# Asking earlier for the keys of step 17, and own buffers with early loads for both halves of the output weights

## The chip, the cores and the metric

The kernel runs on one core of one Trainium2 chip. The metric is the device time of one execution in microseconds, as the median of several runs. A core has five engines that work side by side, each through its own queue in order: TensorE (PE, matrix products), VectorE (DVE), ScalarE (ACT), GpSimd (POOL) and SyncE (SP, which here only asks for transfers). All loads and stores are made by 16 DMA engines; SyncE, ScalarE and GpSimd ask for them.

## The reference, cut to what matters

Attention over a window of neighbours and over block summaries, and behind it a gated layer with two further products. Shapes: 4 batches, 8 heads, 768 rows of 64; 3072 tokens of 512; inner width 1024.

```python
k_sum = k.reshape(B, H, nb, 32, D).max(axis=3)
v_sum = v.reshape(B, H, nb, 32, D).mean(axis=3)
scores_l = where(|i - j| < 16, scale * q @ k.T, -1e9)
scores_s = scale * q @ k_sum.T + log(32)
a = softmax(concatenate([scores_l, scores_s]))
x = a @ concatenate([v, v_sum])          # as (3072, 512)
out = ((x @ w1) * (x @ w2) @ w3) @ w_out
```

## The kernel before, in words

All work is in 32-bit floats; a product is made of three passes over high and low halves of its operands (`products`, L123). The tokens are cut into 6 units of 512 and the heads into 4 pairs, which makes 24 attention steps, numbered 0 to 23. A step loads queries and keys (`load_scores`, L336) and values (`load_values`, L319), adds block summaries to the keys (`gather`, L361, on GpSimd, called through `fill`), makes scores (L376), a softmax over them (`reduce`, `expose`, `invert`, `normalize`, L385 to L414), transposes (L434) and outputs (`outputs`, L449). Queries and keys have two buffers each, so the loads of step p + 2 take the buffers of step p once its scores are done.

The weights w3 and w_out are multiplied with each other at the start (`fold_weights`, L226), into eight tiles `wp`, so that the network is two gate products, their product, and one output product. The first two units go through it in a plain form (`gate`, `project`; the results are copied into tiles `o` and stored, L553 to L556). The other four go in two rounds through a form with seven products of half the size in place of eight (`gates`, `project_fast`, `lanes`, L721 to L753). For that form sums of blocks of the weights are needed. `sums_of_gates` makes them for the gate weights and `sums_of_output` (L948) for the output weights, in two halves c = 0 and 1: `stationary` (L666) loads four blocks `wr` of a half from DRAM (`pR`, written earlier by `spill_high` and `join_wp`, L928 and L931), adds them on VectorE (L690, L692, L696, L701), splits each sum into two parts `sp` (L680 on ScalarE, L121 on VectorE) and stores them (L686). The products in `lanes` go to four accumulators that L759 (ScalarE) and L761 (VectorE) empty into `tmp` and `hr`.

The order of TensorE's and GpSimd's work is written out by hand. Steps 8 to 15 are handled by `lump` (L1288), one at a time, and steps 16 to 23 by `two_steps` (L1325), two at a time. Between the parts of a step, `run` (L997) lets the network go on up to a given number of columns. While it does, `tend` (L982) advances small pieces of side work, one at a time: first the list `tasks`, then the list `background`, whose first entry has to end before the next begins. What SyncE asks for, and what VectorE and ScalarE do outside of the parts with a fixed order, is put into the queues by a scheduler before the run: it takes what it thinks ready, by order in the program, and can take an instruction well ahead of its place.

Names and lines that the change touches:

- `keep_raw` (L466) copies the outputs of steps 8 to 23 into tiles `xraw`. Those of steps 16 to 19 are two tiles with the tag `raw` (two buffers, otherwise used by `load_keys` and `load_blocks`); those of steps 8 to 11 are two with the tag `wf` (six buffers, shared with the softmax tiles `sm`).
- `stationary` has for the output weights four small tiles with the tag `pt` (four buffers). The same tag holds the tiles `o` and `g` of the plain form. Both halves c use it, one after the other.
- `sums_of_output` is put into `background` at the first and the second pair of `two_steps` (`LATER`, L1269). Its loads (L954) are asked for when the background work comes to it.
- `lump(15)` asks for queries and keys of step 17 at its end (L1321), and lets GpSimd add the summaries (L1322).

Of the kernel before, what the change touches and what calls it, by code (L numbers as in the profile page):

```python
# [11 lines left out]
F32 = mybir.dt.float32  # L12
# [8 lines left out]
P = 128  # L21
# [52 lines left out]
def attention_moe(ctx, tc, qG, kW, kT, vP, vW, vB, mask, w1, w2, w3T, wo, out, outT):  # L74
    nc = tc.nc
    B, NPAIR, _, S = kT.shape
    S -= PAD
    NB = S // BLOCK
    U = TOKENS
# [8 lines left out]
    NC = DM // P  # L88
    FQ = w1.shape[2] // 2 // NC
    NF = w1.shape[0] * FQ // P  # L90
# [4 lines left out]
    DH = DO // 2  # L95
# [4 lines left out]
    sb = ctx.enter_context(tc.tile_pool(name="sb", bufs=2))  # L100
# [11 lines left out]
    wp = [sb.tile([P, 2, DO], F32R, name=f"wp{i}", tag="wp", bufs=NF) for i in range(NF)]  # L112

    wS = [[tc.dram_tile([P, 2, KH * FQ], F32, name=f"wS{k}_{q}") for q in range(NQ)] for k in range(NK)]
    pS = {k: [tc.dram_tile([P, 2, 2 * DH], F32, name=f"pS{k}_{c}") for c in range(NF // 4)] for k in range(2, NK - 1)}
    pR = [tc.dram_tile([P, 2, 2, DO], F32, name=f"pR{c}") for c in range(NF // 4)]
# [3 lines left out]
    def low(eng, dst, src, hi):  # L120
        eng.tensor_tensor(dst, src, hi.bitcast(F32), ALU.subtract)  # L121
# [214 lines left out]
    def load_scores(u, p):  # L336

        q = sb.tile([P, U], F32, name="q")
        k = sb.tile([P, NBLK, COLS], F32, name="k")
        eng = nc.gpsimd if u > LAST_UNITS or u == LAST_UNITS and p > 1 else nc.sync  # L340
        eng.dma_start(q, qG[p, :, u * U : (u + 1) * U])
        if u:
            eng.dma_start(k, kW[p, :, u * NBLK : (u + 1) * NBLK])
        return q, k
# [40 lines left out]
    def reduce(u, h, sc, sm, mx):  # L385

        for i in ORDER:
            blk = (u * NBLK + i) % BLOCKS
            j = h * NBLK + i
            nc.vector.tensor_tensor_reduce(  # L390
                out=sm[:, j],
                in0=sc[h][:, i * KR : (i + 1) * KR],
                in1=mask_sb[:, 0 if blk == 0 else 2 if blk == BLOCKS - 1 else 1],
                op0=ALU.add,
                op1=ALU.min,
                scale=-SCALE,
                scalar=3.0e38,
                accum_out=mx[:, 0, j : j + 1],
            )
# [66 lines left out]
    def keep_raw(po, u, c):  # L466

        n, half = divmod(u, 2)
        if (n, half) not in raws:
            if half:  # L470
                home = {"tag": "w12", "bufs": 8} if n == 1 else {"tag": "ring", "bufs": RING}
                t = sb.tile([P, NC, U], F32, name="xraw", **home)
                raws[n, half] = [t[:, i] for i in range(NC)]
            else:
                home = {"tag": "wf", "bufs": 6} if n == 1 else {"tag": "raw", "bufs": 2}
                two = [sb.tile([P, 2, U], F32, name="xraw", **home) for _ in range(NC // 2)]
                raws[n, half] = [two[i // 2][:, i % 2] for i in range(NC)]
        nc.scalar.copy(raws[n, half][c], po[:, :U])
        kept[n, half] = kept.get((n, half), 0) + 1
# [175 lines left out]
    def staggered(works):  # L655

        active = []
        while works or active:
            if works:
                active.append(works.pop(0))  # L660
            active = [work for work in active if next(work, 0)]
            yield 1

    stored = set()

    def stationary(name, load, to_dram, home, apart=False):  # L666


        if apart:
            t = [[sb.tile([P, 512], F32, name="wr", tag="pt", bufs=4) for _ in range(2)] for _ in range(2)]  # L670
        else:
            whole = sb.tile([P, 2, 2, 512], F32, name="wr", tag="ring", bufs=RING)
            t = [[whole[:, i, j] for j in range(2)] for i in range(2)]
        yield from load(t)
        (a11, a12), (a21, a22) = t
        yield 1

        def finished(k, raw):
            to = sb.tile([P, 2, 512], F32R, name="sp", **home)
            nc.scalar.copy(to[:, 0], raw)  # L680
            yield 1
            low(nc.vector, to[:, 1], raw, to[:, 0])
            yield 1
            yield 1
            yield 1
            nc.sync.dma_start(to_dram(k), to.bitcast(F32))  # L686
            stored.add((name, k))

        works = []
        nc.vector.tensor_tensor(a22, a21, a22, ALU.add)  # L690
        yield 1
        nc.vector.tensor_tensor(a21, a11, a21, ALU.subtract)  # L692
        works.append(finished(2, a22))
        next(works[0])
        yield 1
        nc.vector.tensor_tensor(a11, a22, a11, ALU.subtract)  # L696
        works.append(finished(5, a21))
        next(works[0])
        next(works[1])
        yield 1  # L700
        nc.vector.tensor_tensor(a12, a12, a11, ALU.subtract)  # L701
        if apart:
            yield from staggered([*works, finished(4, a11), finished(3, a12)])
            return

        yield from staggered(works)
        for _ in range(3):
            yield 1
        yield from staggered([finished(4, a11), finished(3, a12)])
# [53 lines left out]
    xT, raws, kept, hT, tasks, background = {}, {}, {}, {}, [], []  # L763
# [183 lines left out]

    def sums_of_output(c):  # L948

        def load(t):  # L950
            for h in range(2):
                for i in range(2):
                    to = t[i][h].rearrange("p (j d) -> p j d", d=DH)
                    nc.sync.dma_start(to, pR[c][:, h, :, i * DH : (i + 1) * DH])  # L954
            yield from range(1, 5)

        return stationary("p%d" % c, load, lambda k: pS[k][c], {"tag": "wp", "bufs": NF}, True)

    def network():
        for u in range(2):  # L960
# [21 lines left out]
    def tend():  # L982


        some = False
        for works in (tasks, background):
            while works:
                n = next(works[0], 0)
                if n > 0:
                    return True  # L990
                if n < 0:
                    break
                works.pop(0)
                some = True
        return some

    def run(columns):  # L997

        while given[0] < columns:
            n = next(stream, 0)  # L1000
            if n <= 0:
                if n == 0 or not tend():
                    return
                continue
            given[0] += n
            if given[0] >= tended[0]:
                tended[0] = max(tended[0] + 4.5 * U, given[0])
                tend()

    def place(s):  # L1010
        return divmod(s, NPAIR)
# [3 lines left out]
    def fetch(s):  # L1015
        if s < NS:
            inputs[s] = load_scores(*place(s))

    def fetch_values(s):
        if s < NS:  # L1020
            values[s] = load_values(*place(s))
# [5 lines left out]
    def fill(s):  # L1027
        if s < NS:
            gather(*place(s), inputs[s][1])
# [159 lines left out]
    with tc.manual_schedule(engines={engines.SP}):  # L1189
        start_loads(0)  # L1190
        active, pairs, t = [], [], [-1]
        while units or active or pairs or delayed or WORK or t[0] <= FIRST[-1]:
# [20 lines left out]
            if t[0] in FIRST[: NPAIR + 1]:  # L1213
                n = FIRST.index(t[0])
# [37 lines left out]
    SINGLE = LAST_UNITS * NPAIR  # L1252
# [3 lines left out]
    PAIRS = range(SINGLE // 2, NS // 2)  # L1256
# [3 lines left out]
    def begins(m):  # L1260
# [6 lines left out]
        15: [lambda: flow_in(4), lambda: moving_x(1, 2)],  # L1267
    }
    LATER = {  # L1269
        (PAIRS[0], 0): [lambda: background.append(sums_of_output(0))],  # L1270
        (PAIRS[0], 1): [lambda k=k: moving_x(1, k) for k in range(3, NK)],
        (PAIRS[0] + 1, 0): [lambda: background.append(sums_of_output(1))],
    }

    for i in range(NF):
# [12 lines left out]
    def lump(p):  # L1288

        if p == NFIRST:  # L1290
            load_batch()
            fill(p)
        else:
            fetch_means(*place(p - 1), values[p - 1])
            fetch(p + 1)
        with tc.manual_schedule(engines=VECTOR):
            t, home = sms.pop(p - 2)
            pt = evacuate(transposes(t), "V" if p in (12, 13) else "A", home)
            u, sm, mx, sc = begin(p)
            reduce(u, 0, sc, sm, mx)  # L1300
            if p > NFIRST + 1:
                expose(0, sm, mx)
                reduce(u, 1, sc, sm, mx)
        run(given[0] + (24 if p == NFIRST + 1 else 18) * U)
        with tc.manual_schedule(engines=VECTOR):
            finish_step(p - 2, pt, **SPARE)
            if p <= NFIRST + 1:
                expose(0, sm, mx)
                reduce(u, 1, sc, sm, mx)
            expose(1, sm, mx)  # L1310
            invert(mx)
            normalize(sm, mx)
            fill(p + 1)
            reduce_batch()
        fetch_values(p)
        for work in EXTRA.get(p, ()):
            work()
        run((given[0] + UP_TO[p]) / 2)
        load_batch()
        if p == SINGLE - 1:  # L1320
            fetch(p + 2)  # L1321
            fill(p + 2)  # L1322
        run(UP_TO[p])

    def two_steps(m):  # L1325
# [133 lines left out]
```

## Time and profile before

| | us |
|---|---|
| median of 3 runs | 514.2 |
| lowest and highest run | 513.1, 516.83 |
| the profiled execution | 517.44 |
| its span, first to last instruction | 515.7 |
| TensorE busy in the span | 486.8 |
| VectorE, ScalarE, GpSimd busy | 357.2, 317.3, 62.5 |

The rows further below come from the profiled execution. Times in them are microseconds from the start of the span. A row of a timeline has its start, its length, the engine, the line of the kernel, the operation, what it writes and reads, and how many instructions are merged in it; in square brackets stands how long the engine had been idle before it and what ended that. SPq is the queue of SyncE; its length is that of the asking, not of the transfer. A row of the waits has the total in us, how often, and the longest. Shares and clocks are in tenths or as fractions; a granted clock of 1.00 is 2.4 GHz, and the lower level is 1.2 GHz.

### The profile page before, as it was taken

What the parts mean: (1) busy time and instruction counts of PE and PEld (TensorE: products, weight loads), DVE (VectorE), ACT (ScalarE), POOL (GpSimd) and SP (SyncE); (2) the same over time, 40 slices, a digit from 0 to 9 for tenths busy, and PEclk for the clock granted to TensorE, in tenths of its full rate; (3) what the DMA queues carried; (4) which work ended last, traced back from release to release, by engine and by line L of the source; (5) the groups of instructions that cost most, each with busy time, mean ns of one, the idle gap of its engine ahead of it and who ended that gap; (6) DMA issues with size and microseconds to landing.
All of it is one profiled execution on the core that took longest, in us unless ns stands there. A gap on an engine that the chain in (4) does not pass through costs nothing.

```text
span 515.7 us, 10541 instructions
## 1 busy us (share of the span) xinstructions
PE 486.8 (94%) x3804; PEld 394.0 (76%) x3804; DVE 357.2 (69%) x873; ACT 317.3 (62%) x882; POOL 62.5 (12%) x121
## 2 busy tenths in 40 slices
PE   1889999999999999999699999799999999999997
PEld 0667778888877777777488887588788888888886
DVE  5969886997604969876269792779969019229972
ACT  5589865776718878888496767578734421522720
POOL 1034522000212010000212021022000000000000
PEclk9999999999999999999799999899999999999999
DMA  8998698998699988889978799896769766556762
GB/s 344 411 409 263 225 353 284 363 402 345 198 292 242 326 244 261 282 299 317 331 231 288 254 343 340 275 308 196 219 186 263 245 196 200 185 190 203 205 187 98
DMA packets 56068, 139.29 MB, mean 270 GB/s; under 512 B 6224, under 2 KB 19280, under 8 KB 53456
## 3 DMA queue, kind: packets, MB, share of 16 engines
q1 hardware_dynamic: 51600, 127.44, 73.1%
q0 software_dynamic: 3264, 9.08, 7.2%
q10 hardware_dynamic: 1152, 2.10, 1.1%
q8 instruction: 30, 0.49, 0.4%
q14 instruction: 22, 0.18, 0.1%
HBM read 105.89 MB, written 32.70 MB: 269 GB/s over the span
## 4 chain that ended last, share of the span: by engine, by line
PE 75%; ACT 10%; DMA 8%; DVE 6%; issue 1%; SPq 0%; POOL 0%; ACTq 0%; POOLq 0%; DVEq 0%
PE ln L741 40%; PE mm L125 26%; PE po L457 4%; PE sc L376 3%; DMA wr<-pR 3%; ACT sm L404 2%; DVE wf L206 2%; DMA v<-in_vW_dram 2%; DMA k<-in_kW_dram 2%; PE tp L434 1%; ACT w L220 1%; DVE w L121 1%; ACT wf L176 1%; ACT hT L644 1%; DMA raw<-in_vB_dram 1%; DMA wraw<-in_wo_dram 1%
## 5 line engine op out<-in xcount | busy, mean ns | idle before, releaser
L741 PE MATMUL ln<-xT,ws 128*128 128x512 f32 x672 | 158.2, 396 | 4.6 <-DVE tmp L761 4.6
L741 PEld LDWEIGHTS ln<-xT,ws 128*128 128x128 f32 x672 | 127.6, 191 | 32.4 <-DVE tmp L761 4.7
L125 PE MATMUL mm<-x,w 128*128 128x512 f32 x384 | 90.6, 393 | 0.0
L125 PEld LDWEIGHTS mm<-x,w 128*128 128x128 f32 x384 | 71.1, 188 | 16.0 <-issue 0.8
L404 ACT ACTIVATE sm<-sm,mx 128x120 f32<-128x120 f32 x192 | 73.9, 393 | 9.9 <-DVE mx L390 9.7
L741 PE MATMUL ln<-hT,ws 128*128 128x512 f32 (+1 forms) x348 | 77.6, 383 | 0.1
L741 PEld LDWEIGHTS ln<-hT,ws 128*128 128x128 f32 x348 | 63.6, 188 | 13.3 <-ACT tmp L759 0.5
L761 DVE TENSOR_TENSOR tmp<-ln,tmp 128x512 f32<-128x512 f32 (+1 forms) x53 | 35.8, 680 | 52.4 <-PE ln L741 38.3
L125 PE MATMUL mm<-w,w 128*128 128x512 f32 x192 | 50.3, 412 | 14.6 <-ACT w L220 11.9
L644 ACT CAST hT<-hr 128x512 fp32r<-128x512 f32 x56 | 32.2, 624 | 41.6 <-DVE hr L818 33.0
L390 DVE CUSTOM_DVE_ANT_0 sm<-sc,mask_sb 128x120 f32<-128x120 f32 x192 | 41.4, 277 | 21.6 <-PE sc L376 21.6
L125 PEld LDWEIGHTS mm<-w,w 128*128 128x128 f32 x192 | 36.2, 194 | 25.6 <-ACT w L220 12.7
L125 PE MATMUL mm<-wp,h 128*128 128x512 f32 x192 | 46.3, 395 | 0.0
L125 PEld LDWEIGHTS mm<-wp,h 128*128 128x128 f32 x192 | 35.4, 188 | 8.4 <-issue 0.5
L414 ACT ACTIVATE sm<-sm,mx 128x120 f32<-128x120 f32 x128 | 38.8, 386 | 2.5 <-DVE mx L410 2.4
L121 DVE TENSOR_TENSOR hT<-hr,hT 128x512 fp32r<-128x512 f32 x56 | 36.0, 699 | 4.0 <-ACT hT L644 3.9
L404 ACT ACTIVATION_READ_ACCUMULATOR sm<-sm,mx 128x1 f32 x192 | 37.8, 197 | 0.0
L121 DVE TENSOR_TENSOR w<-wf,w 128x1024 fp32r<-128x1024 f32 (+1 forms) x22 | 25.6, 1166 | 8.2 <-ACT w L220 8.2
L376 PE MATMUL sc<-k,q 64*64 64x120 f32 x768 | 25.7, 274 | 5.7 <-POOL k L363 5.6
L220 ACT CAST w<-wf 128x1024 fp32r<-128x1024 f32 (+1 forms) x22 | 21.5, 976 | 14.7 <-DVE wf L206 13.4
L759 ACT COPY tmp<-ln 128x512 f32<-128x512 f32 x32 | 18.8, 588 | 18.6 <-PE ln L741 18.3
L363 POOL COPY k<-ks 128x96 f32<-128x96 f32 (+1 forms) x32 | 9.9, 322 | 151.6 <-DMA k<-in_kW_dram 135.1
(72 smaller groups left out, 571.8 us busy)
## 6 DMA issues: line engine op xcount, KB each, us to landing
ws<-wS SPq DMA_DIRECT2D x56, 512.0 KB
wraw<-in_w3T_dram SPq DMA_DIRECT2D x8, 1024.0 KB
wraw<-in_w_dram SPq DMA_DIRECT2D x8, 1024.0 KB
wS<-sp SPq DMA_DIRECT2D x16, 512.0 KB
ws<-pS SPq DMA_DIRECT2D x16, 512.0 KB
raw<-in_kT_dram SPq DMA_DIRECT2D x16, 392.0 KB
wS<-w SPq DMA_DIRECT2D x12, 512.0 KB
ws<-pW SPq DMA_DIRECT2D x24, 256.0 KB
```

Of the source, the lines that this page charges most:

```text
L121: eng.tensor_tensor(dst, src, hi.bitcast(F32), ALU.subtract)
L125: nc.tensor.matmul(acc, lhsT=a, rhs=b, start=first and i == 0, stop=last and i == len(terms) - 1)
L220: nc.scalar.copy(t[:, 0, some], f[:, some])
L376: nc.tensor.matmul(sc[h][64 * g : 64 * g + 64, i * KR : (i + 1) * KR], lhsT=q[rows, i * P + 64 * g : i * P + 64 * g + 64], rhs=k[rows, i, ...
L390: nc.vector.tensor_tensor_reduce(out=sm[:, j], in0=sc[h][:, i * KR : (i + 1) * KR], in1=mask_sb[:, 0 if blk == 0 else 2 if blk == BLOCKS - ...
L404: nc.scalar.activation(sm[:, j], sm[:, j], AF.Exp, bias=mx[:, 0, j : j + 1], scale=-1.0, accum_out=mx[:, 1, j : j + 1])
L414: nc.scalar.activation(sm[:, j], sm[:, j], AF.Copy, scale=mx[:, 2, j : j + 1])
L457: nc.tensor.matmul(po[cols, at : at + 64], lhsT=v[:KR, g, i, cols], rhs=pt[g][:, (h * NBLK + i) * 64 : (h * NBLK + i + 1) * 64], start=Tru ...
L644: nc.scalar.copy(dst[0], src)
L741: nc.tensor.matmul(bank[:, cols], lhsT=x, rhs=y[:, cols], start=c + j == 0 and (split or k in o.first), stop=c == steps - 1 and j == 2 and ...
L759: nc.scalar.copy(parts[to][:, cols], got)
L761: nc.vector.tensor_tensor(parts[to][:, cols], got, parts[more][:, cols], ALU.add)
```

## The change

Three edits. Queries and keys of step 17 are asked for in `lump(15)` right behind the scores of step 15, and GpSimd's part follows behind the loads of the values. `sums_of_output` gets its buffers and asks for its four loads at once when it is called, and puts only the adding, splitting and storing into `background`, with two steps less of waiting (`range(1, 3)` for `range(1, 5)`); the second half takes two double tiles with the tag `raw`, the first half keeps `pt`. The outputs of steps 16 to 19 are kept in `wf` in place of `raw`.

```diff
@@ keep_raw
-                home = {"tag": "wf", "bufs": 6} if n == 1 else {"tag": "raw", "bufs": 2}
-                two = [sb.tile([P, 2, U], F32, name="xraw", **home) for _ in range(NC // 2)]
+                two = [sb.tile([P, 2, U], F32, name="xraw", tag="wf", bufs=6) for _ in range(NC // 2)]
@@ stationary
-    def stationary(name, load, to_dram, home, apart=False):
-        if apart:
-            t = [[sb.tile([P, 512], F32, name="wr", tag="pt", bufs=4) for _ in range(2)] for _ in range(2)]
+    def stationary(name, load, to_dram, home, apart=None):
+        if apart is not None:
+            t = apart
...
-        if apart:
+        if apart is not None:
@@ sums_of_output
-        def load(t):
-            for h in range(2):
-                for i in range(2):
-                    to = t[i][h].rearrange("p (j d) -> p j d", d=DH)
-                    nc.sync.dma_start(to, pR[c][:, h, :, i * DH : (i + 1) * DH])
-            yield from range(1, 5)
-        return stationary("p%d" % c, load, lambda k: pS[k][c], {"tag": "wp", "bufs": NF}, True)
+        if c:
+            two = [sb.tile([P, 2, 512], F32, name="wr", tag="raw", bufs=2) for _ in range(2)]
+            t = [[two[i][:, j] for j in range(2)] for i in range(2)]
+        else:
+            t = [[sb.tile([P, 512], F32, name="wr", tag="pt", bufs=4) for _ in range(2)] for _ in range(2)]
+        for h in range(2):
+            for i in range(2):
+                to = t[i][h].rearrange("p (j d) -> p j d", d=DH)
+                nc.sync.dma_start(to, pR[c][:, h, :, i * DH : (i + 1) * DH])
+        background.append(stationary("p%d" % c, lambda _: range(1, 3), lambda k: pS[k][c], {"tag": "wp", "bufs": NF}, t))
@@ LATER
-        (PAIRS[0], 0): [lambda: background.append(sums_of_output(0))],
+        (PAIRS[0], 0): [lambda: sums_of_output(0)],
...
-        (PAIRS[0] + 1, 0): [lambda: background.append(sums_of_output(1))],
+        (PAIRS[0] + 1, 0): [lambda: sums_of_output(1)],
@@ lump
                 reduce(u, 1, sc, sm, mx)
+        if p == SINGLE - 1:
+            fetch(p + 2)
         run(given[0] + (24 if p == NFIRST + 1 else 18) * U)
...
         fetch_values(p)
+        if p == SINGLE - 1:
+            fill(p + 2)
         for work in EXTRA.get(p, ()):
             work()
         run((given[0] + UP_TO[p]) / 2)
         load_batch()
-        if p == SINGLE - 1:
-            fetch(p + 2)
-            fill(p + 2)
         run(UP_TO[p])
```

## Rows read from the trace of the kernel before

**Rows 1.** The page's first part: busy us, share of span, instructions.

```profile
PE 486.8 (94%) x3804; PEld 394.0 (76%) x3804; DVE 357.2 (69%) x873; ACT 317.3 (62%) x882; POOL 62.5 (12%) x121
```

**Rows 2.** Waits of TensorE: total us, times, longest.

```profile
PE sc L376 <- POOL k L363: 5.6, 1, 5.6
PE ln L741 <- DVE tmp L761: 4.6, 1, 4.6
```

**Rows 3.** TensorE's timeline around the scores of steps 15 to 17.

```profile
231.92 1.05 PE L376 MATMUL sc<-k,q 64*64 64x120 f32 x32
...
243.25 1.05 PE L376 MATMUL sc<-k,q 64*64 64x120 f32 x32
249.94 1.88 PE L376 MATMUL sc<-k,q 64*64 64x120 f32 x32 [5.64 <-POOL k L363]
251.75 5.71 PE L741 MATMUL ln<-xT,ws 128*128 128x512 f32 x18
...
259.08 5.05 PE L741 MATMUL ln<-xT,ws 128*128 128x512 f32 x21
...
265.14 13.21 PE L741 MATMUL ln<-xT,ws 128*128 128x512 f32 x57
```

**Rows 4.** TensorE's timeline ahead of the second wait and behind it.

```profile
294.36 9.18 PE L741 MATMUL ln<-xT,ws 128*128 128x512 f32 x39
...
325.90 10.05 PE L741 MATMUL ln<-xT,ws 128*128 128x512 f32 x36 [4.56 <-DVE tmp L761]
```

**Rows 5.** Windows: busy us and counts, then granted clock, DMA share, GB/s.

```profile
240.00:252.00 12.00, 6.36 (x93) 5.01 (x93) 5.12 (x23) 7.38 (x29) 1.54 (x4) 0.83 1.00 317
...
326.00:346.00 20.00, 20.00 (x192) 16.53 (x193) 16.20 (x56) 13.81 (x50) 3.04 (x6) 0.91 0.92 283
```

**Rows 6.** Timeline of SyncE's queue: requests for transfers.

```profile
231.68 1.72 SPq L359 DMA_DIRECT2D v<-vS  x2
...
237.64 0.57 SPq L341 DMA_DIRECT2D q<-in_qG_dram  x1
...
241.47 0.35 SPq L343 DMA_DIRECT2D k<-in_kW_dram  x1
...
248.55 3.73 SPq L954 DMA_DIRECT2D wr<-pR  x4
...
307.05 3.06 SPq L954 DMA_DIRECT2D wr<-pR  x3
```

**Rows 7.** Chain of work that ended last: start, us, what.

```profile
227.88 8.22 DMA v<-in_vW_dram
236.15 5.26 DMA raw<-in_vB_dram
241.47 8.05 DMA k<-in_kW_dram
...
311.43 13.03 DMA wr<-pR
```

**Rows 8.** GpSimd's timeline.

```profile
185.37 1.77 POOL L935 DMA_DIRECT2D pR<-wp  x2 [0.22 <-issue]
...
249.66 0.39 POOL L363 COPY k<-ks 128x48 f32<-128x48 f32 x2 [17.47 <-DMA k<-in_kW_dram]
```

**Rows 9.** VectorE's timeline around the two additions at L690.

```profile
260.66 0.69 DVE L690 TENSOR_TENSOR wr<-wr 128x512 f32<-128x512 f32 x1 [2.58 <-DMA wr<-pR]
...
267.54 1.90 DVE L640 TENSOR_TENSOR xraw<-xraw 128x512 f32<-128x512 f32 x3 [1.25 <-ACT xraw L478]
269.35 0.69 DVE L761 TENSOR_TENSOR tmp<-ln,tmp 128x512 f32<-128x512 f32 x1
...
324.55 0.69 DVE L690 TENSOR_TENSOR wr<-wr 128x512 f32<-128x512 f32 x1 [9.01 <-DMA wr<-pR]
```

**Rows 10.** ScalarE's timeline: last output copy, last casts of the first half.

```profile
242.81 0.56 ACT L555 COPY o<-mm 128x512 f32<-128x512 f32 x1
...
304.06 1.14 ACT L680 CAST sp<-wr 128x512 fp32r<-128x512 f32 x2
```

## The prediction

> **What bounds the kernel now.** I read the page's first part, then the waits of TensorE, then its timeline around each wait, then the timelines of whoever it waited for. TensorE is busy 486.8 of 515.7 us [rows 1], so a change pays only where TensorE stands still. Most of its idle time is the start of the program, which the change doesn't touch. Afterwards it waits twice for long: 5.6 us for the keys that GpSimd completes, and 4.6 us for VectorE's additions at L761 [rows 2].
>
> The first wait stands between the scores of step 16 and step 17: the former end at 244.30, the latter begin at 249.94, 5.64 us later [rows 3]. The clock then falls: the granted clock averages 0.83 over 240 to 252, a mix of the 2.4 and the 1.2 GHz level [rows 5]. So step 17's scores take 1.88 us where step 16's took 1.05, and the first 18 products 5.71 us [rows 3]. Where no stall is near, 39 such products take 9.18 us [rows 4], 0.235 us each, so 18 take 4.24. The stall's whole price is 5.64 + 0.83 + 1.47 = 7.94 us.
>
> The second wait stands before the products at 325.90, 4.56 us [rows 4]. The 36 products behind it take 10.05 us against 36 x 0.235 = 8.47, with the clock at 0.91 over 326 to 346 [rows 4, 5]: 1.58 us more. Price: 6.14 us. Together the two cost 14.08 us.
>
> Why the first: the queue of SyncE asks for step 17's queries at 237.64 and for its keys only at 241.47 [rows 6]. The scores of step 15, whose buffers they take, end at 232.97 [rows 3]. The chain shows the delay: values asked for at 227.88 land 8.22 us later, only then a block of values (`raw`) starts, 5.26 us, only when that has landed does the request for the keys go out, 8.05 us [rows 7]. No buffer joins these three; SyncE's requests wait for the landing of earlier ones. Then GpSimd fills in the summaries, 0.39 us for two copies, and TensorE starts [rows 8].
>
> Why the second: VectorE stands 9.01 us at L690 for the second half of the output weights, and the evacuation L761 that TensorE needs is behind it [rows 9]. The last of that half's four loads was asked for at 311.43 and landed 13.03 us later [rows 7]; the first three went out from 307.05 [rows 6]. They take over the four `pt` buffers of the first half, whose last casts begin at 304.06 [rows 10].
>
> **The change part by part.** *Keys of step 17.* No instruction is added; queries and keys (two requests, 0.57 and 0.35 us of the queue [rows 6]) move to right behind step 15's scores. They pass two blocks of `raw` and whatever requests for `ws` stand between. They queue behind the mean loads at 231.68 to 233.40 [rows 6]. The wait for earlier landings stays, so I put the keys at 236.15, the moment when the first block of `raw` was let out of the chain [rows 7]. With the 8.05 us that they took they land at 244.20; 0.08 us of issue and 0.39 us of copies make 244.67, which is 0.37 us after the scores of step 16. One bound is no wait left: with the blocks behind them less is in flight ahead. The other, if the blocks keep their place and only the values of step 15 and the `ws` loads are passed: about two microseconds later, 2.3 us of wait. I take 0.4, nearer to the rows. What is pushed back is the two blocks; their reductions come in VectorE's queue ahead of step 16's reductions, and TensorE has the 18 products before it needs those.
>
> The Trainium skill (DMA: Bandwidth & Descriptors, Anatomy of one DMA) gives a lone GpSimd-path transfer about 2.0 us plus its bytes over 436 GB/s; as an estimate from that page 368 KB land in 2.9 us, and the keys would land at 239 with nothing left of the wait. No run here shows a lone load of this size, and the 8.05 us of the row rule, since the queue is full there.
>
> GpSimd's `fill` of step 17 moves ahead with its keys. Nothing stands between it and the next request on that queue, which needs the scores of step 16 anyway.
>
> *First half of the output weights.* Its four loads (256 KB each, 3.73 us of SyncE's queue for the four [rows 6]) stand earlier in the program, at the start of the pair of steps 16 and 17 and no longer behind all the background work before them, but their buffers are the `pt` tiles that the output copies `o` use. The last `o` is copied at 242.81 [rows 10], and the loads went out at 248.55 [rows 6], though the data in DRAM were joined by about 190 (requests at 185.37 [rows 8]). So they can gain at most some 5 us. The adds of the half come two steps of the background earlier.
>
> This is where I expect a part of the gain to be given back. VectorE already waits 2.58 us at L690 for these loads, until 260.66 [rows 9]; TensorE doesn't notice. Between that and the first L761 at 269.35 lie 7.4 us of work of VectorE's (8.69 less an idle of about 1.25). TensorE needs that L761 for its fourth product. Each of the seven products is 24 matmuls (four banks, two chunks, three terms), so the fourth begins after 72: 18, 21 and then 33 of the 57 from 265.14 [rows 3], about 272.8. With the first stall gone it is 7.94 sooner, 264.9. If L690 begins at T, L761 ends at T + 7.4 + 0.69, so TensorE waits T - 256.8. T is 252 at best (loads out at 243.4, landing after the 8.4 us that they took from their last issue: no wait) and, left where it was, 260.66: 3.9 us. The second half's 1 MB now stands in the same stretch, where the DMA engines move 317 GB/s at a share of 1.00 [rows 5]: up to 3.3 us more, so T = 264 and 7.2 us at the worst. I take 2.0 us: the loads go out sooner by most of what they can.
>
> *Second half.* Its loads get buffers of their own, `raw`, free once VectorE has reduced the last blocks of values, just ahead of step 16's reductions. They leave the time from 307 to 312 [rows 6, 7] and come at the pair of steps 18 and 19 or, as their data and buffers are ready, well before it. The 9.01 us at L690 go, and with them the 6.14 us. What is late next there? After 326 the waits of TensorE have no further entry of that length [rows 2], so nothing stands close behind. The bound on the other side is a new wait of VectorE for the same loads elsewhere, counted above.
>
> *The raw outputs of steps 16 to 19* go into two `wf` buffers instead of `raw`. Six `wf` hold four softmax tiles and two raws; the raws of steps 8 to 11 have been used up by then, since TensorE is at its fourth product or later. The later softmax tiles must take the buffers of steps 16 and 17, which TensorE reads just ahead of the scores of 20 and 21 on its own queue. That order hides it: 0 us; without the cover it would cost a wait of two steps' small matmuls, some 2 us by the 1.05 us of a step's scores [rows 3].
>
> **Sum.** 14.08 - 0.4 - 2.0 = 11.7 us off. The profiled execution took 517.44 us (span 515.7), so 505.7 by its own time. The median of the runs is 514.2, 3.2 us less; taken off that it is 502.5, which I give as the time.
>
> **Rivals.** *The wait moves to the first half* (0.20): T = 264, TensorE waits 7.2 us before the fourth product and loses the clock again (1.58): gain 14.08 - 0.4 - 8.8 = 4.9, 509.3 us. For it: VectorE is in order, it waits there already, and TensorE comes 8 us sooner. Against: the loads can go out sooner, and the idle of 1.25 us closes.
>
> *The keys are not earlier* (0.08), so the change doesn't do what it says: the request still waits for the same landing. Then only 6.14 less a small loss of 2.0 is won: 510.1 us. For: three requests in the chain waited for landings and not for buffers. Against: the request moves ahead of two of those links.
>
> *The output copies lose their buffers* (0.07), the slow side: the first half's loads, now early in the program, take `pt` buffers before the last `o`. That copy then waits until a load's tile is released, and with it the accumulator that TensorE wants at 245.35, when the scores of step 17 would end. The tiles were released after the casts, 305.2 [rows 10]: 59.9 us of stall, 514.2 - 14.1 + 59.9 = 560 us. It decides from a release later than 245.35 + 14.08 = 259.4; sooner, the kernel stays ahead. Against: before, the loads also ran far ahead of their use, yet went out only after the last `o` was copied.
>
> **How the numbers follow.** The forecast, 500 to 506, has 0.58. The rivals have 0.35, and 0.07 is for smaller mishaps up to no change. One per cent, 5.1 us, is about what a measurement of this kernel can tell from no change. Faster by more than that (under 509.1): the forecast, nearly half of the first rival, and a little of the rest, 0.75; slower 0.08; same 0.17. The range goes down to 499, the lowest run of before, 513.1, less all of 14.08. Upward it goes to 511, which takes in the first two rivals; beyond lie the slow case and mishaps.
>
> **What would show it.** Right: keys of step 17 asked for by about 236 and no wait of TensorE at them above 1 us; the second half's loads out before 290; no 9 us at L690; the clock at 1.0 in both places. The 2.0 us would show as a TensorE wait on L761 near 265. Wrong: the keys' request still past 240; a new wait of VectorE on `wr` that TensorE feels for more than 4 us; an output copy that waits for a `pt` buffer.

## The result, and the profile after

The changed kernel takes 512.36 us (median of 21 runs, 508.73 to 515.02), the kernel before 516.74 us on the same chip (21 runs, 512.31 to 518.69). The ratio is 0.9907, with a 95% interval of 0.9885 to 0.9929: 0.93% faster, or 4.8 us of 516.74 (the two medians differ by 4.4). The forecast was 11.7 us, and as a time 502.5 with a range of 499 to 511, which 512.36 exceeds. The 514.2 us from which it was taken off is the median of three runs; that alone makes 2.5 us of the distance between 502.5 and 512.36. The other 7.3 us are gain that didn't come.

The profiled execution's span is 511.2 us against 515.7, 4.5 us less, so it can be used to see where the gain stayed. Lines of the kernel after bear numbers one lower from L475 to L948: L741 is now L740, L761 L760, L690 L689. Those of [rows 1, 2] first: the page's first part, kernel after.

```profile
PE 487.2 (95%) x3804; PEld 393.5 (77%) x3804; DVE 357.7 (70%) x873; ACT 317.2 (62%) x882; POOL 61.3 (12%) x121
```

The waits of TensorE, kernel after (total us, times, longest):

```profile
PE ln L740 <- DVE tmp L760: 4.9, 1, 4.9
...
PE ln L740 <- ACT hr L758: 0.8, 1, 0.8
```

The wait of 5.6 us for the keys is gone. A wait of 4.6 us for the addition L761 has its match, 4.9 us, and it looks as if nothing had been done about that one. The timeline shows that it isn't the same wait. TensorE's timeline, kernel after:

```profile
243.78 1.87 PE L376 MATMUL sc<-k,q 64*64 64x120 f32 x64
245.58 4.42 PE L740 MATMUL ln<-xT,ws 128*128 128x512 f32 x18
...
257.69 5.08 PE L740 MATMUL ln<-xT,ws 128*128 128x512 f32 x21
263.59 3.03 PE L740 MATMUL ln<-xT,ws 128*128 128x512 f32 x12 [0.83 <-ACT hr L758]
271.50 8.54 PE L740 MATMUL ln<-xT,ws 128*128 128x512 f32 x24 [4.88 <-DVE tmp L760]
...
322.96 8.49 PE L740 MATMUL ln<-xT,ws 128*128 128x512 f32 x36
```

Against [rows 3]: the scores of steps 16 and 17 now run in one piece (64 instructions from 243.78), and the 18 products behind them take 4.42 us where they took 5.71. Against [rows 4]: the 36 products that waited 4.56 us and then took 10.05 now wait for nothing and take 8.49. So both stalls of before went, with their clock losses. But 72 products after the scores of step 17 (18, 21, 21 and 12) a new stall of 4.88 us stands at 271.50, ahead of the fourth product, and the 24 products behind it take 8.54 us, 2.90 more than 24 x 0.235 = 5.64. The windows of the kernel after (busy us and counts, then granted clock, DMA share, GB/s) show where the clock is lost: it is 1.00 where [rows 5] have 0.83 and 0.91, and below 1.00 around the new stall.

```profile
240.00:252.00 12.00, 12.00 (x163) 9.72 (x162) 6.89 (x39) 10.01 (x38) 2.63 (x6) 1.00 1.02 317
252.00:280.00 28.00, 22.29 (x114) 17.00 (x112) 19.48 (x34) 18.37 (x55) 2.30 (x7) 0.88 0.95 314
326.00:346.00 20.00, 20.00 (x227) 16.58 (x226) 14.36 (x51) 10.96 (x46) 3.04 (x6) 1.00 0.94 304
```

The balance: won 7.94 + 6.14 = 14.08, as predicted. Given back: 4.88 + 0.83 of waits and 2.90 of clock behind the first, 8.61. Behind the wait of 0.83 nothing of the clock is lost: the granted clock is 1.00 from 263.5 to 267. That leaves 5.47. The scores of step 15, ahead of everything that the change touches, already begin 0.53 us later in this execution (232.45 against 231.92), which leaves 4.94 beside the 4.5 of the spans.

What did TensorE wait for? VectorE's timeline, kernel after:

```profile
258.74 0.69 DVE L689 TENSOR_TENSOR wr<-wr 128x512 f32<-128x512 f32 x1 [10.44 <-DMA wr<-pR]
259.35 0.68 DVE L121 TENSOR_TENSOR sp<-wr,sp 128x512 fp32r<-128x512 f32 x1
...
266.17 0.69 DVE L689 TENSOR_TENSOR wr<-wr 128x512 f32<-128x512 f32 x1 [1.13 <-DMA wr<-pR]
266.90 0.69 DVE L691 TENSOR_TENSOR wr<-wr 128x512 f32<-128x512 f32 x1
267.62 0.69 DVE L695 TENSOR_TENSOR wr<-wr 128x512 f32<-128x512 f32 x1
268.35 0.69 DVE L700 TENSOR_TENSOR wr<-wr 128x512 f32<-128x512 f32 x1
268.96 1.89 DVE L639 TENSOR_TENSOR xraw<-xraw 128x512 f32<-128x512 f32 x3
270.77 0.68 DVE L760 TENSOR_TENSOR tmp<-ln,tmp 128x512 f32<-128x512 f32 x1
```

L689 appears twice. The first is the first half, at 258.74. The second, at 266.17, is the second half: its additions, before at 324.55 [rows 9], came ahead with its loads and stand between the first half and the L760 that TensorE needs. From the start of the first L689 to that of L760 it is 12.03 us, before 260.66 to 269.35 = 8.69. A line that stands twice in a stretch where it stood once is the sign to look for.

### The profile page after: what moved, and what is told of

Read it like the earlier page. It is cut to its first block, busy times and chain, and to the rows that moved or that the text cites. A ratio compares the mean times of both kernels' runs of the same rounds, so it can differ in the third digit from the quotient of the medians.

```text
span 511.2 us, 10548 instructions
## 1 busy us (share of the span) xinstructions
PE 487.2 (95%) x3804; PEld 393.5 (77%) x3804; DVE 357.7 (70%) x873; ACT 317.2 (62%) x882; POOL 61.3 (12%) x121
## 4 chain that ended last, share of the span: by engine, by line
PE 76%; ACT 8%; DMA 7%; DVE 5%; issue 1%; POOL 0%; SPq 0%; POOLq 0%; DVEq 0%; ACTq 0%
PE ln L740 42%; PE mm L125 26%; PE po L457 4%; PE sc L376 3%; DMA k<-in_kW_dram 3%; PE tp L434 2%; DMA wr<-pR 2%; ACT wf L176 2%; ACT sm L404 2%; DVE wf L206 2%; ACT w L220 1%; DVE w L121 1%; DMA wraw<-in_w_dram 1%; DVE wf L203 1%; DMA wraw<-in_wo_dram 1%
## 5 line engine op out<-in xcount | busy, mean ns | idle before, releaser
L740 PE MATMUL ln<-xT,ws 128*128 128x512 f32 x672 | 158.8, 396 | 5.7 <-DVE tmp L760 4.9
L740 PEld LDWEIGHTS ln<-xT,ws 128*128 128x128 f32 x672 | 127.2, 191 | 34.3 <-DVE tmp L760 5.3
L740 PE MATMUL ln<-hT,ws 128*128 128x512 f32 (+1 forms) x348 | 77.6, 383 | 0.2 <-ACT tmp L758 0.2
L740 PEld LDWEIGHTS ln<-hT,ws 128*128 128x128 f32 x348 | 63.6, 188 | 13.3 <-ACT tmp L758 0.6
L760 DVE TENSOR_TENSOR tmp<-ln,tmp 128x512 f32<-128x512 f32 (+1 forms) x53 | 35.5, 674 | 53.8 <-PE ln L740 39.0
L121 DVE TENSOR_TENSOR hT<-hr,hT 128x512 fp32r<-128x512 f32 x56 | 35.6, 681 | 4.0 <-ACT hT L643 3.9
L121 DVE TENSOR_TENSOR w<-wf,w 128x1024 fp32r<-128x1024 f32 (+1 forms) x22 | 25.6, 1167 | 8.2 <-ACT w L220 8.2
L176 ACT ACTIVATE wf<-wraw 128x1024 f32<-128x1024 f32 (+1 forms) x22 | 23.2, 1065 | 7.7 <-DMA wraw<-in_wo_dram 3.5
L758 ACT COPY tmp<-ln 128x512 f32<-128x512 f32 x32 | 18.8, 588 | 14.4 <-PE ln L740 13.3
```

The source lines that it names most:

```text
L176: nc.scalar.activation(f[:, some], words[:, some, 1].bitcast(F32), AF.Prelu, scale=2.0**-112, alpha=-(2.0**32),)
L740: nc.tensor.matmul(bank[:, cols], lhsT=x, rhs=y[:, cols], start=c + j == 0 and (split or k in o.first), stop=c == steps - 1 and j == 2 and ...
L758: nc.scalar.copy(parts[to][:, cols], got)
L760: nc.vector.tensor_tensor(parts[to][:, cols], got, parts[more][:, cols], ALU.add)
```

## The experiments

Two theories of the 4.88 us. **A, additions**: VectorE works in order, the second half's four additions (266.17 to 268.96, 2.8 us) and the wait for their loads (1.13) stand at its head just when TensorE wants L760. **B, traffic**: the second half's loads share the stretch with the first half's and bring these late. Each run's ratio is to the kernel before, run on the same chip beside it. Additions that are "held" wait for a copy: GpSimd copies one column of a block onto itself, so that the additions that read the block must come behind that copy in time. The copy itself is a small instruction on an engine that is busy for 61.3 of 511.2 us.

**Each part alone.** Only the keys (the kernel before with the move of queries, keys and `fill`):

> Only the keys of step 17 are asked for early; the output weights stay as they were. Theory A (the give-back of the changed kernel comes from the additions of the second half standing ahead of the evacuations on VectorE): without them the loads of the first half go out as before, VectorE's first evacuation comes some 2 us late for a TensorE that is 6 us sooner, and the whole 7.9 us of the first stall less 1 to 2 us is kept: ratio to before 0.986 to 0.990, with the old 4.6 us stall near 318 still there. Theory B (the stretch is bound by its transfers, whoever's additions stand where): TensorE waits some 5 us again near 265 to 270, little is left: ratio 0.994 to 1.000.

Measured: 513.28 us, ratio 0.9925 (0.9896 to 0.9954), between the forecasts of the two theories; the interval reaches into both, so the time doesn't decide. Only the weights (the kernel after with the keys where they were):

> Only the output weights' buffers and early loads; the keys of step 17 as before, so the first stall of 5.6 us stays. Theory A: the four additions of the second half (2.9 us) and their wait now stand ahead of the evacuations, where there were 2.8 us of room; TensorE waits 1 to 3 us near 273 and the 6.1 us of the second stall go: ratio 0.990 to 0.995. Theory B: 1 MB more in the same stretch at about 320 GB/s is 3.3 us; TensorE waits 3 us or more: ratio 0.993 to 1.000. The two differ little here; the size is wanted for the sum of the parts.

Measured: 511.52 us, ratio 0.9901 (0.987 to 0.9932), at the edge of A's forecast; the TensorE wait near 273 that both theories expected (1 to 3 us, or more) didn't come. TensorE's timeline with the keys alone:

```profile
267.22 7.33 PE L741 MATMUL ln<-xT,ws 128*128 128x512 f32 x24 [1.78 <-DVE tmp L761]
```

The same view with the weights alone, around the first stall and at the fourth product:

```profile
248.64 1.88 PE L376 MATMUL sc<-k,q 64*64 64x120 f32 x32 [4.70 <-DMA out_dram<-o]
250.45 6.30 PE L740 MATMUL ln<-xT,ws 128*128 128x512 f32 x18
...
264.44 13.21 PE L740 MATMUL ln<-xT,ws 128*128 128x512 f32 x57
```

The 4.70 us are the old wait for the keys, though the row names a store: GpSimd's first copy for these keys begins 0.28 us before the scores, at 248.36, as it did in [rows 8] (249.66 before 249.94).

VectorE's timeline with the keys alone, its first addition of the first half:

```profile
259.13 0.69 DVE L690 TENSOR_TENSOR wr<-wr 128x512 f32<-128x512 f32 x1 [7.52 <-DMA v<-vS]
```

And with the weights alone, the first addition of either half:

```profile
257.38 0.69 DVE L689 TENSOR_TENSOR wr<-wr 128x512 f32<-128x512 f32 x1 [5.10 <-ACT tmp L758]
...
264.48 0.69 DVE L689 TENSOR_TENSOR wr<-wr 128x512 f32<-128x512 f32 x1 [0.75 <-DMA wr<-pR]
```

With the keys alone no load of the second half is in the stretch, and still the first half's addition begins at 259.13, no earlier than with both (258.74). That gives B no support, though single starts of this addition scatter, as two runs below show. With the weights alone the second half's additions stand in the stretch (264.48), and TensorE doesn't notice: it comes late itself, by the 4.70 us of the first stall, and the 57 products run without a gap. So the parts gain 0.75% and 0.99% alone and 0.93% together. Both live on the same slack of VectorE ahead of the fourth product: one part brings TensorE sooner, the other puts 4 us of work and waiting on VectorE, and each alone fits or nearly fits (1.78 us of wait with the keys alone, none with the weights alone).

**The second half's additions held** behind the scores of step 18; its loads stay where the change put them.

```diff
@@ sums_of_output (kernel after)
+        if c:
+            held = t[1][1][:, :1]
+            HELD[PAIRS[0] + 1] = [lambda: nc.gpsimd.tensor_copy(held, held)]
         background.append(stationary("p%d" % c, lambda _: range(1, 3), lambda k: pS[k][c], {"tag": "wp", "bufs": NF}, t))
...
+    HELD = {}
...
@@ two_steps
             fetch(a + 2)
+            for work in HELD.pop(m, ()):
+                work()
```

> The changed kernel, with the second half loaded as early as in it, but its additions held back by a copy of one column on GpSimd that stands behind the scores of step 18. Theory A: VectorE still waits 10 us for the first half, but the first evacuation comes 4 us sooner; TensorE's 4.9 us wait falls to about 1 us and the clock stays up: 5 to 7 us less than the changed kernel, ratio to before 0.978 to 0.982. Theory B: the transfers are the same, so the time is that of the changed kernel, ratio 0.989 to 0.992.

Measured: 507.24 us, ratio 0.9812 (0.9782 to 0.9842). VectorE's timeline of this run:

```profile
259.00 0.69 DVE L689 TENSOR_TENSOR wr<-wr 128x512 f32<-128x512 f32 x1 [10.62 <-DMA wr<-pR]
...
267.03 0.68 DVE L760 TENSOR_TENSOR tmp<-ln,tmp 128x512 f32<-128x512 f32 x1
...
281.74 0.68 DVE L689 TENSOR_TENSOR wr<-wr 128x512 f32<-128x512 f32 x1
```

TensorE's timeline of this run, at the fourth product:

```profile
267.94 5.98 PE L740 MATMUL ln<-xT,ws 128*128 128x512 f32 x24 [1.06 <-DMA ws<-wS]
```

The first half begins where it did, at 259.00, but L760 comes 3.7 us sooner, and the 4.88 us at TensorE and the 2.90 us of clock behind it are gone; 1.06 us for another load (`ws`) are left. The gain doubles, and the interval lies wholly under that of the change. The ratio is in A's forecast and outside B's. This is theory A, with the second half's loads still in the stretch.

**The second half's loads held as well**, by a GpSimd memset of one column of each block; loads and additions both come behind the scores of step 18.

```diff
@@ sums_of_output (kernel after)
+        if c:
+            for row in t:
+                for block in row:
+                    nc.gpsimd.memset(block[:, :1], 0.0)
@@ LATER
-        (PAIRS[0] + 1, 0): [lambda: sums_of_output(1)],
@@ two_steps, HELD = {PAIRS[0] + 1: [lambda: sums_of_output(1)]}
             fetch(a + 2)
+            for work in HELD.pop(m, ()):
+                work()
```

> The changed kernel, with the loads of the second half held back as well (their tiles are first touched on GpSimd behind the scores of step 18). Theory A: as e3, ratio 0.978 to 0.982, if VectorE doesn't stand for those loads at their new place; they take 8 to 13 us to land, and each us by which the additions stand too early there is lost again. Theory B: with 1 MB less ahead of it the first half lands 2 to 3 us sooner, ratio 0.980 to 0.985, and better than e3 by as much as the traffic costs.

Measured: 515.29 us, ratio 0.9958 (0.9931 to 0.9984): most of the gain is gone, and neither theory's range has it. A's condition, that VectorE doesn't stand for those loads at their new place, wasn't met. VectorE's timeline of this run:

```profile
261.29 0.69 DVE L689 TENSOR_TENSOR wr<-wr 128x512 f32<-128x512 f32 x1 [12.16 <-DMA wr<-pR]
...
291.87 0.69 DVE L689 TENSOR_TENSOR wr<-wr 128x512 f32<-128x512 f32 x1 [7.16 <-DMA wr<-pR]
```

TensorE's timeline of this run, behind that addition:

```profile
293.21 5.53 PE L740 MATMUL ln<-xT,ws 128*128 128x512 f32 x15 [5.84 <-DVE hr L760]
```

Without the second half's traffic the first half begins at 261.29, not sooner. This alone doesn't refute B: a run below asks for the same loads in the same order up to here, and there the first half begins at 255.37. The two are 5.9 us apart, more than the 3.3 us at which the traffic was priced. So the stall of 4.88 us is A's by the run with the additions held, and whether the traffic moves the first half's start by a few us stays open. And the additions, left to the scheduler, stand at VectorE's head 7.16 us before their loads have landed, at the new place, as they did at 324.55 before. In these kernels the wait goes where the loads go. Left to the scheduler, the addition came to the head before its load had landed each time (by 10.44 and 1.13 us at the two L689 of the kernel after, 7.16 here, 9.01 in [rows 9]).

**Both halves' additions held**, the first half's behind the scores of step 18, the second's behind those of step 20 (the edit held for c = 0 too, `HELD[PAIRS[0] + 1 + c]`):

> The changed kernel, with the loads as early as in it, and the additions of both halves held back on GpSimd: the first half's behind the scores of step 18, the second half's behind those of step 20. Theory A (what VectorE has at the head of its queue while the loads are on their way sets the time): VectorE no longer stands some 10 us near 250, the last 1 to 3 us of waits of TensorE near 263 to 268 go too, and the clock stays up: 2 to 3 us less than with the second half alone held, ratio to before 0.974 to 0.978. Theory B (transfers): 2 MB are loaded in the same stretch as in the changed kernel; nothing beyond the 0.981 of the run with the second half held, or worse.

Measured: 508.44 us, ratio 0.9844 (0.980 to 0.9889), less gain than A's 0.974 to 0.978; by its time alone it would fit B's "0.981, or worse". **The first half's additions alone held**:

> The mirror of the run with the second half's additions held: only those of the first half are held back behind the scores of step 18, those of the second half stay ahead of the evacuations. Theory A: four additions in place of eight stand there again, but behind loads that land 3 to 6 us later than the first half's (262 to 265 against 259); the first evacuation comes at 267 to 270: 1 to 4 us better than the changed kernel, ratio 0.983 to 0.988. Theory B: as the changed kernel, 0.989 to 0.992.

Measured: 510.25 us, ratio 0.9878 (0.9844 to 0.9912), between the change and the held second half, in A's forecast, though the interval reaches B's. **The halves' buffers exchanged**, beside the held second half: the first takes the two `raw` tiles and need not wait for the last store of an output copy, the second takes `pt`:

```diff
@@ sums_of_output (second half's additions held)
-        if c:
+        if not c:
             two = [sb.tile([P, 2, 512], F32, name="wr", tag="raw", bufs=2) for _ in range(2)]
```

> As the run with the additions of the second half held, but with the buffers of the halves exchanged: the first half is loaded into raw, so its last load no longer waits for the store of the last output tile. Theory A with that store as the reason for the late landing: the additions of the first half begin 2 to 4 us sooner than at 259.0, and TensorE's waits near 264 and 268 (1.9 us together) shrink below 0.5: ratio 0.976 to 0.980. If it is the queue of transfers as a whole that sets the landing, the additions begin at 258 to 260 again and the ratio stays at 0.981.

Measured: 506.35 us, ratio 0.9801 (0.9765 to 0.9837), which doesn't part the two forecasts. The additions did begin 2.5 us sooner (256.52), but TensorE's waits didn't shrink below 0.5 us. TensorE's timeline at the fourth product, both halves held:

```profile
268.90 5.71 PE L740 MATMUL ln<-xT,ws 128*128 128x512 f32 x24 [3.08 <-DMA ws<-wS]
```

The first half alone held:

```profile
270.22 7.21 PE L740 MATMUL ln<-xT,ws 128*128 128x512 f32 x24 [4.25 <-DVE tmp L760]
```

The buffers exchanged, second half held:

```profile
268.14 5.72 PE L740 MATMUL ln<-xT,ws 128*128 128x512 f32 x24 [2.32 <-DMA ws<-wS]
```

With only the first half held, the second half's additions take its place at VectorE's head (L689 at 264.89 after 8.78 us of standing) and TensorE waits 4.25. There is less to add than in the kernel after, and it hardly helps, since VectorE can't begin before the last load has landed. With VectorE out of the way in the other two, L760 is done by 263.88 and 265.77, and what is late next is a load, `ws`, the weights of the fourth product. It had been hidden behind VectorE's 4.88. The chain of the run with both halves held shows why `ws` is late:

```profile
256.50 8.61 DMA wS<-sp
...
265.12 3.64 DMA ws<-wS
```

`wS<-sp` is the store (L685) of sums of the gate weights. By the chain, the request for `ws` stands at SyncE until that store has landed, 8.61 us here. With the second half alone held the store takes 4.20 us in the chain, with the buffers exchanged as well 4.02.

**Loads and additions both out of the stretch, the additions behind the landing.** That `ws` load is asked for by SyncE behind the second half's loads. So: these loads behind the scores of step 18, their additions held behind the scores of step 20.

```diff
@@ sums_of_output (the run with the loads held)
-        background.append(stationary("p%d" % c, lambda _: range(1, 3), lambda k: pS[k][c], {"tag": "wp", "bufs": NF}, t))
+        if c:
+            held = t[1][1][:, :1]
+            HELD[PAIRS[0] + 2] = [lambda: nc.gpsimd.tensor_copy(held, held), lambda: background.append(stationary("p%d" % c, lambda _: range(1, 3), lambda k: pS[k][c], {"tag": "wp", "bufs": NF}, t))]
+        else:
+            background.append(stationary("p%d" % c, lambda _: range(1, 3), lambda k: pS[k][c], {"tag": "wp", "bufs": NF}, t))
```

> The changed kernel, but the second half's four loads go out behind the scores of step 18 (about 279) and its additions may start only behind the scores of step 20, after the loads have landed; the first half is as in the changed kernel. Theory A (VectorE stands in order at whichever addition the scheduler put ahead, so loads and additions must both leave the stretch, and the additions must come after the landing): no wait of TensorE on L760 above 1 us near 271, none of 5.8 us near 293 as when only the loads were held; span 505 to 508, ratio to before 0.977 to 0.983. Rival C (what is left near 268 in the versions with held additions, 1.1 to 3.1 us for ws, comes from the second half's loads standing ahead of ws in SyncE's queue): that wait falls under 0.5 us here. Rival D (the ws loads are late because of the store of the same sums shortly before, whatever else is in the queue): 1 to 3 us for ws stay.

> The run before (second half's loads behind the scores of step 18, its additions behind those of step 20), with the buffers of the halves exchanged besides: the first half in raw, the second in pt. The first half's loads need not wait for the last output store then: VectorE starts L689 at 256 to 257 rather than at 258.7 to 261.3. Theory C: with nothing of the second half in the queue, ws comes in time, no wait of TensorE above 1 us between 245 and 330, span 503 to 505, ratio 0.973 to 0.979. Theory D: 2 to 3 us for ws stay near 268, ratio 0.979 to 0.982.

Measured: 506.85 us, ratio 0.9791 (0.9752 to 0.983), and with the buffers exchanged 505.8 us, ratio 0.9768 (0.9733 to 0.9804). The profiled execution of the first is the fastest of its six runs (504.20 us), that of the second is near its median (505.65). The waits of TensorE in the first of the two, the whole list:

```profile
PE mm L125 <- ACT w L220: 12.0, 2, 11.5
PE mm L125 <- DVE w L121: 2.6, 4, 1.2
PE po L457 <- ACT pt L442: 0.3, 1, 0.3
PE po L457 <- ACT pt L444: 0.2, 1, 0.2
```

No L740 stands in it: neither the wait for `ws` nor any for L760, here or at 293. With the buffers exchanged 0.28 us for `ws` are left. SyncE's queue in the first of the two, the same store and the first request for `ws` behind it:

```profile
256.69 0.33 SPq L685 DMA_DIRECT2D wS<-sp  x1
257.07 2.13 SPq L359 DMA_DIRECT2D v<-vS  x4
260.08 0.34 SPq L785 DMA_DIRECT2D ws<-wS  x1
```

The request goes out 3.4 us after that of the store, where with both halves held it took 8.6. The fairest pair is that with the buffers exchanged: the store is asked for at 259.29 and at 258.98, and TensorE waits 2.32 and 0.28 us for `ws`. So rival D of the expectations falls (the store is there, but no wait above 0.3 us), and what C forecast came: the `ws` wait of 1.1 to 3.1 us goes with the second half's loads. C's reason isn't shown as it was put. The store is the link that the chain names, and these loads lengthen it; whether by their place in SyncE's queue or by their traffic in the DMA engines isn't separated, since these two runs take away both. The two differ from each other, and from the run with held additions, by less than their intervals, so whether the exchange gains anything isn't settled. It moved the first L689 from 259.00 to 256.52 with the second half's loads in the stretch; without them it began at 255.37 unexchanged and at 256.20 exchanged:

```profile
255.37 0.69 DVE L689 TENSOR_TENSOR wr<-wr 128x512 f32<-128x512 f32 x1 [7.63 <-DMA wr<-pR]
```

This is the start that stands against the 261.29 above. The last version is the fastest by its median, 2.3% under the kernel before, and its interval (up to 0.9804) lies wholly under that of the change (from 0.9885).

## Why the prediction was wrong

**What held.** The price of the two stalls, 14.08 us, was won in full: the clock is 1.00 in both windows of [rows 5], and the products behind run at 0.236 to 0.246 us. The raw outputs in `wf`, put at 0, show in no wait of TensorE. The order of the mechanism held too: the loads leave the time around 307, the 9 us at L690 go, and part of the gain comes back as a TensorE wait on the first half's L761, in the place that was named (needed at 264.9 by the forecast; TensorE was free for it at 271.50 - 4.88 = 266.62, later by the 0.5 us of this execution, the 0.83 on L758 and smaller pieces). T, the start of the first half's additions, was put at 258.8 (the 2.0 us taken, on 256.8) and came at 258.74. That close a hit is luck: the 2.0 was a choice between 0 and 7.2, and two runs with the same requests up to there began at 261.29 and 255.37. The bound "T is 252 at best" is also summed wrongly: it counts the 8.4 us from the first request at 243.4, though they were measured from the end of the last, 3.73 us later, so it is 255.5. It changes nothing in the sum, since TensorE waits only from 256.8 on.

**The keys**: put at 0.4 us of residual wait, measured none. SyncE's queue, kernel after, beside [rows 6]:

```profile
235.08 1.22 SPq L276 DMA_DIRECT2D raw<-in_vB_dram  x2
236.39 0.39 SPq L341 DMA_DIRECT2D q<-in_qG_dram  x1
236.87 0.38 SPq L343 DMA_DIRECT2D k<-in_kW_dram  x1
...
238.97 3.82 SPq L325 DMA_DIRECT2D v<-in_vW_dram  x3
...
245.74 0.39 SPq L957 DMA_DIRECT2D wr<-pR  x1
...
249.52 0.95 SPq L957 DMA_DIRECT2D wr<-pR  x2
...
254.03 0.36 SPq L957 DMA_DIRECT2D wr<-pR  x1
...
255.01 0.88 SPq L957 DMA_DIRECT2D wr<-pR  x2
```

The request didn't pass the two blocks of `raw`, as I had it, but it no longer waits for one of them to land: the values (L325), which used to be asked for before it, come behind. It goes out at 236.87 (forecast 236.15, in an execution that is 0.5 us later there), and the chain of the kernel after has its landing:

```profile
236.87 7.13 DMA k<-in_kW_dram
...
260.93 5.15 DMA wr<-pR
266.17 0.70 DVE wr L689
```

The keys land at 244.00, GpSimd is done at 244.54, and the scores of step 16 end at 244.83: 0.3 us to spare. The last two rows are the second half: its last load, and the addition that waited for it. The Trainium skill (DMA: Bandwidth & Descriptors, Anatomy of one DMA) gives a lone GpSimd-path transfer about 2.0 us plus its bytes over 436 GB/s, an estimate of 2.9 us for these 368 KB; no run here shows a lone one. This one, asked for by SyncE, took 7.13, with the DMA engines at a share of 0.89 meanwhile, so there the row of before was the better guide.

**The step that failed** is "Between that and the first L761 at 269.35 lie 7.4 us of work of VectorE's", with which TensorE's wait became T - 256.8. The 7.4 was the work of before. The change puts the second half's additions into the same stretch of VectorE's queue, and the forecast counted of that half only the loads, as traffic that could move T. T came where it was put. The term became 12.03: 7.4, four additions of 2.8, 1.13 of waiting for their last load, and 0.7 for a split (L121 at 259.35) and a reciprocal that used to run ahead of L690. So L760 ended 4.6 us later than forecast, and the sign of being wrong that the prediction named came: "a new wait of VectorE on `wr` that TensorE feels for more than 4 us" (4.88). The run with the additions held takes these out and gets most of it back (267.03 for 270.77 with T at 259.00 for 258.74).

The prediction did say that the instructions "come at the pair of steps 18 and 19 or, as their data and buffers are ready, well before it", and called "a new wait of VectorE for the same loads elsewhere" counted. It wasn't: that place priced the loads in the DMA engines and not the instructions behind them on VectorE. It listed what the keys' requests pass on SyncE, but not what the additions get in front of on VectorE.

**A second term left out** is the clock. A wait of 2.0 us was put down at 2.0. The wait that came cost 2.90 more in the 24 products behind it, at a granted clock of 0.64 from 271 to 280, as the two that were removed had cost clock; in the forecast that price was on the winning side alone (0.83, 1.47 and 1.58) and in the first rival.

**The rivals.** The measured gain is that of the first, the wait that moves to the first half (4.9 us forecast there, 4.4 by the medians), with its 0.20. But its mechanism, first-half loads later by the second half's traffic (T = 264), is not what happened: T was 258.74 with those loads, and 259.13, 261.29 and 255.37 without them in this place. "The keys are not earlier" and "the output copies lose their buffers" didn't occur; the last output copies begin at 236.53 and 243.34 without a wait.

## What to carry to other kernels

When loads are brought forward, ask who reads them: the readers come forward too, and on an engine that works in order a reader that reaches the head before its load has landed stops everything behind it. Price the stretch they move into by the whole queue of that engine, from the row that frees it to the row that the bound engine needs, and count the clock behind a new stall as well as behind an old one. Two edits that each gain alone can use up the same slack, so run them singly before adding their prices. And a start that lies 5.9 us apart in two executions of the same requests can't show an effect of 3.3.

## What was not expected of the hardware

The length of a stall said little of what the clock took behind it. After 4.56 us of waiting 36 products took 1.58 us too long [rows 4]; after 4.88 us in the kernel after 24 products took 2.90 too long. With the first half held 24 products took 7.21 after 4.25, 1.57 too long; with the keys alone 7.33 after 1.78, 1.69 too long at a granted clock of 0.77. After 3.08 us for `ws`, with both halves held, they took 5.71 at a granted clock of 1.00, almost nothing over 5.64.

In SyncE's queue a request that waited for a store held back those behind it. The kernel after asks for three of the first half's loads by 250.5 and for the fourth only at 254.03, and the second half's next two follow from 255.01; the waits of SyncE's queue name the store of an output copy.

```profile
SPq L957 <- DMA out_dram<-o: 4.3, 2, 3.0
```

That the store was the only reason for the late landing isn't shown: with the second half's loads away, L689 began at 255.37 in one run and at 261.29 in another without the exchange of buffers.
